# Softcap attention and gated FFN: the weights' sign word from GpSimd, end rows loaded from ScalarE's queue

## The chip, the cores and the metric

The kernel runs on one core of a Trainium2 chip. The metric is the device time of one execution in microseconds (us); less is better. Times of executions that are compared come from the same chip.

## What is computed

A softcapped attention over 4 batches, 12 heads, 448 positions and 64 dimensions feeds a gated FFN over the 1792 tokens (768 wide, 1536 hidden). The weights of the FFN are float64 in memory.

```python
scores = cap * np.tanh(scale * np.matmul(q, k.transpose(0, 1, 3, 2)) / cap)
attn = np.exp(scores - np.max(scores, axis=-1, keepdims=True))
attn = attn / (np.sum(attn, axis=-1, keepdims=True) + 1e-09)
x = np.matmul(attn, v)            # then heads side by side: (1792, 768)
out = (1 / (1 + np.exp(-(x @ w_gate))) * (x @ w_val)) @ w_out
```

## The kernel before

**Stages.** `_emit` runs two generators against each other. `attention_of` (here `_bounded_attention`, since the cap is 30) makes the attention of a batch in 6 pairs of heads; `moe(b)` makes the FFN of batch b. Batch 0's attention runs alone; then moe(0) beside the attention of batch 1, and so on, and moe(3) alone. TensorE and ScalarE take their instructions in the order in which the two generators emit them; the order on VectorE, GpSimd and SP's DMA queue is a scheduler's, with some operations raised in priority.

**Pairs.** For a pair n the scores come out transposed, keys on the partitions; ScalarE takes tanh (L416) and exp (L424). Pairs 0 to 11 (`direct`) multiply float32 tiles; pairs 6 to 11, batch 1, have their keys in 4 chunks of 112 (`even`), the others in chunks of 128. From pair 12 on the exponentials are split into a rounded part `ph` and a remainder `pl` (`emit_P`, L426 to L444), and `a` is summed by GpSimd (L436 to L438). Before that the buffers of tags ph and pl hold only pair 0's transposed k and q. T is the split of the transposed k and q of the next pair: ScalarE rounds it (L209), VectorE makes the remainder (L215), and the next pair's scores wait for it. L530 and L534 or L538 divide by the sum.

**Weights.** There are 36 units of 128 x 768: 24 of w_gate and w_val in turn, 12 of w_out. Each is loaded once as float64 (`load_w64`, L754) and made into float32 in `convert_w` by one ScalarE and three VectorE operations:

```python
nc.scalar.activation(x, top.bitcast(F32), AF.Copy, scale=2.0 ** -112)
nc.vector.tensor_scalar(xi, xi, 3, None, ALU.logical_shift_left)
nc.vector.scalar_tensor_tensor(xi, top, -2 ** 31, xi, ALU.bitwise_and, ALU.bitwise_or)
nc.vector.scalar_tensor_tensor(half, low.bitcast(U32), 2.0 ** -29, half, ALU.mult, ALU.add)
```

They are L771 to L774, on one of two buffers in `pair0`. `split_w` then makes wspl, the rounded part by GpSimd (L207) and the remainder by VectorE (L215; by GpSimd for the first 4 units). `prepare_w(u)` asks for the conversion of unit u + 5. Units 0 to 3 are converted in batch 0's attention at pairs 2 to 5 (`PLAN`), the others in moe(0), one after the other as TensorE reaches unit u; all are stored to memory and loaded again by SP for the later batches (L836, L845), into four wspl buffers, or, for some odd units, as one float32 tile that ScalarE and VectorE split again.

**FFN.** In moe(b), f counts 12 blocks; per block two units (gate, value) of 18 matmuls each (L900), ScalarE's tanh (L943), VectorE's product (L946) and its split into g_spl. Then 12 units of w_out, in two halves of the columns, in three chunks of 128 rows (L1028). The last 64 rows of a batch don't fill a chunk: batches 0 to 2 store their part of g_spl as grest (L959), and the last batch puts all batches' ends into `rest`, four tiles in the buffers of tag t, as two more chunks. At the start of moe(3) the loads rest <- grest (L917), three for each tile, go out on SP's queue; the scheduler has them among SP's loads of batch 2's last weights.

Of the kernel before, what the change touches and what calls it, by code (L numbers as in the profile page):

```python
# [9 lines left out]
F32 = mybir.dt.float32  # L10
F32R = mybir.dt.float32r
I32 = mybir.dt.int32
# [4 lines left out]
ALU = mybir.AluOpType  # L17
AX = mybir.AxisListType

P = 128  # L20
# [230 lines left out]
def _bounded_attention(o, x_done):  # L251
# [13 lines left out]

    nc, c, ap = o.nc, o.c, o.ap
    o.early = 4
    o.out_tag = ("v_spl", 2)
    o.rest_tags = (("t", 2, 2), ("t", 2, 2))
    B, H, S, D, NF, NC, R = o.B, o.H, o.S, o.D, o.NF, o.NC, o.REST  # L270
# [155 lines left out]
    def emit_P(n, j):  # L426

        t = Pt[n][:, j]
        ph = ap.tile([P, NC, S], F32R, tag="ph", bufs=1, name=f"ph{n}_{j}")
        pl = ap.tile([P, NF, S], F32R, tag="pl", bufs=1, name=f"pl{n}_{j}")  # L430
# [8 lines left out]
        f = a[0:D]  # L439
# [181 lines left out]
def _general_attention(o, x_done):  # L621

    nc, c, ap = o.nc, o.c, o.ap
    o.early = 36
    o.out_tag = ("T", 2)
# [7 lines left out]
    for n in range(o.B * o.NPAIR):  # L633
        b, p = divmod(n, o.NPAIR)
# [68 lines left out]
def _emit(tc, ctx, c, attention_of, q, k, v, w_gate, w_val, w_out, out):  # L703
    nc = tc.nc
# [7 lines left out]
    W64 = 3  # L712
    WRAW = 2
    KEEP = 4
    AHEAD = 3
# [16 lines left out]
    UN = KD * P  # L732
# [24 lines left out]
    def convert_w(u):  # L757
# [13 lines left out]
        nc.scalar.activation(x, top.bitcast(F32), AF.Copy, scale=2.0 ** -112)  # L771
        nc.vector.tensor_scalar(xi, xi, 3, None, ALU.logical_shift_left)
        nc.vector.scalar_tensor_tensor(xi, top, -2 ** 31, xi, ALU.bitwise_and, ALU.bitwise_or)
        nc.vector.scalar_tensor_tensor(  # L774
# [118 lines left out]
    def moe(b):  # L893
# [14 lines left out]
        if b == B - 1:  # L908
            tiles = []
            for tag, bufs, n in o.rest_tags:  # L910
                r = ap.tile([P, n, 2, NR // P, KR, P], F32R, tag=tag, bufs=bufs, name=f"rest{len(tiles)}")
                tiles += [r[:, i] for i in range(n)]
            for x, r in enumerate(tiles):
                for at, d in enumerate(g_rest):
                    n = P if at < b // GR else b % GR * R
                    for i in (range(2) if n < P else [slice(0, 2)]):
                        nc.sync.dma_start(  # L917
                            out=r[:, i, at, :, 0:n].bitcast(F32),
                            in_=d[:, i, x * KR:(x + 1) * KR, 0:n].bitcast(F32),
                        )  # L920
                rest.append(r)
        u = u0

        for f in range(KF):
# [8 lines left out]
            for which in range(2):  # L933
# [10 lines left out]
                else:  # L944
                    with tc.high_priority(offset=AHEAD_OF):
                        nc.vector.scalar_tensor_tensor(gate, gate, 1.0, ps, ALU.add, ALU.mult)  # L946
                    o.hi("p", g_spl[:, 0, f, :], gate)
                    o.lo("v", g_spl[:, 1, f, :], gate, g_spl[:, 0, f, :])
        moe1_done[b] = True
        flush_x()  # L950
# [155 lines left out]
```

## Time and profile before

| | |
|---|---|
| runs shown | 760.33, 760.93, 762.32 us; median 760.93 |
| profiled execution, its own time | 760.87 us |
| its span, first to last instruction | 759.1 us |
| mean granted TensorE clock | 0.994 of full speed |
| TensorE busy, matmuls | 742.4 us, 98% |
| VectorE / ScalarE / GpSimd busy | 510.0 / 356.1 / 248.3 us (67 / 47 / 33%) |
| moved by DMA | 151.78 MB, 200 GB/s |

Times in the profile count from the start of the span. Batch 0's attention fills about 0 to 72 us, moe(0) 72 to 265, moe(1) to 435, moe(2) to 601, moe(3) to the end. A matmul's end is modelled, so a busy TensorE is not one at its peak; a share is a mean over stages with different limits. Line numbers are those of the kernel before.

### The profile page before, as it was taken

The numbers are of one execution on the slowest core, as the hardware profiler recorded it, in microseconds if no ns is written. First come the engines' busy times: TensorE is split into PE (matmuls) and PEld (weight loads), VectorE is DVE, ScalarE is ACT, GpSimd is POOL, SyncE is SP. The second block draws the span as 40 slices with busy tenths as digits, with TensorE's granted clock in tenths as the row PEclk, the third lists the DMA queues.
The fourth block names the chain that finished last, engine by engine and source line by source line (L and its number), as shares of the span: only waits on it lengthen the run. The fifth ranks groups of instructions, "written<-read, shape, count | busy, mean of one in ns | idle before, by whom it ended". The sixth has DMA issues, their size and how long they took to land.

```text
span 759.1 us, 10351 instructions
## 1 busy us (share of the span) xinstructions
PE 742.4 (98%) x3900; PEld 642.1 (85%) x3900; DVE 510.0 (67%) x538; ACT 356.1 (47%) x392; POOL 248.3 (33%) x255
## 2 busy tenths in 40 slices
PE   8999999999999799999999999999999999999997
PEld 6556877777788788888899988888998999999996
DVE  3798889978997748988986738899878032322000
ACT  5987565465537156755574155655561011111000
POOL 1364332323333435454545305455462000000000
PEclk9999999999999899999999999999999999999999
DMA  5878798988799674544566854533369855463551
GB/s 127 216 194 214 273 300 264 300 244 264 236 286 349 223 265 118 153 151 139 156 174 224 296 198 134 144 106 123 125 195 307 303 171 176 158 190 103 175 168 57
DMA packets 128391, 151.78 MB, mean 200 GB/s; under 512 B 80716, under 2 KB 106828, under 8 KB 128332
## 3 DMA queue, kind: packets, MB, share of 16 engines
q1 hardware_dynamic: 125468, 147.02, 61.9%
q10 hardware_dynamic: 2864, 4.00, 1.5%
q8 instruction: 33, 0.54, 0.3%
q14 instruction: 26, 0.21, 0.1%
HBM read 118.75 MB, written 31.46 MB: 198 GB/s over the span
## 4 chain that ended last, share of the span: by engine, by line
PE 63%; DMA 2%; DVE 1%; SPq 0%; issue 0%; ACT 0%
PE h L900 35%; PE o L1028 17%; PE sc L413 4%; DMA wspl<-wd 2%; PE pv L484 2%; PE pv L483 2%; PE dn L522 1%; PE pv L485 1%; PE tp L360 1%; PE tp L244 1%; DVE rd L530 0%; SPq L845 0%; DVE ph L215 0%; DVE wspl L215 0%; DVE a L440 0%
## 5 line engine op out<-in xcount | busy, mean ns | idle before, releaser
L900 PE MATMUL h<-xspl,wspl 128*128 128x448 f32 x1728 | 377.1, 372 | 0.0
L900 PEld LDWEIGHTS h<-xspl,wspl 128*128 128x128 f32 x1728 | 321.3, 188 | 41.7 <-issue 15.5
L1028 PE MATMUL o<-wspl,gspl 128*128 128x384 f32 x864 | 162.8, 342 | 6.3 <-DVE wspl L215 3.9
L1028 PEld LDWEIGHTS o<-wspl,gspl 128*128 128x128 f32 x864 | 152.7, 190 | 12.2 <-DVE wspl L215 4.2
L416 ACT ACTIVATE t<-sc,scale 128x896 f32<-128x896 f32 (+1 forms) x90 | 85.9, 1002 | 32.5 <-PE sc L413 32.2
L207 POOL TENSOR_SCALAR gspl<-gate 128x448 fp32r<-128x448 f32 x48 | 43.1, 897 | 162.2 <-DVE gate L946 162.2
L424 ACT ACTIVATE t<-t,capv 128x1792 f32<-128x1792 f32 (+2 forms) x48 | 83.2, 1738 | 10.1 <-issue 6.4
L215 DVE TENSOR_TENSOR wspl<-pair,wspl 128x768 fp32r<-128x768 f32 x68 | 76.9, 1132 | 15.0 <-POOL wspl L207 12.5
L946 DVE SCALAR_TENSOR_TENSOR gate<-gate,h 128x448 f32<-128x448 f32 x48 | 29.6, 616 | 74.1 <-PE h L900 64.1
L943 ACT ACTIVATE gate<-h 128x448 f32<-128x448 f32 x48 | 26.1, 543 | 105.6 <-PE h L900 105.1
L530 DVE RECIPROCAL rd<-rd 128x448 f32<-128x448 f32 x24 | 70.7, 2947 | 5.1 <-ACT rd L503 2.7
L413 PE MATMUL sc<-T 64*128 64x448 f32 (+1 forms) x522 | 66.5, 382 | 1.1 <-DVE T L215 1.1
L207 POOL TENSOR_SCALAR wspl<-pair 128x768 fp32r<-128x768 f32 x36 | 35.5, 986 | 94.1 <-DVE pair L774 48.3
L413 PEld LDWEIGHTS sc<-T 64*128 64x128 f32 (+1 forms) x522 | 44.9, 181 | 20.7 <-issue 11.8
L209 ACT ACTIVATE wspl<-pair 128x768 fp32r<-128x768 f32 x36 | 30.4, 844 | 66.7 <-PE h L900 66.5
L436 POOL TENSOR_TENSOR a<-t 128x448 f32<-128x448 f32 x24 | 31.3, 1304 | 67.4 <-ACT t L424 32.3
L1002 DVE TENSOR_SCALAR osb<-o 128x384 f32<-128x384 f32 x16 | 8.6, 555 | 62.8 <-PE o L1028 62.7
L209 ACT ACTIVATE ph<-t 128x1792 fp32r<-128x1792 f32 x24 | 40.8, 1698 | 14.0 <-PE pv L485 14.0
L215 DVE TENSOR_TENSOR pl<-t,ph 128x1344 fp32r<-128x1344 f32 x24 | 46.3, 1929 | 0.4
L215 DVE TENSOR_TENSOR gspl<-gate,gspl 128x448 fp32r<-128x448 f32 x48 | 41.3, 860 | 7.2 <-POOL gspl L207 6.9
L774 DVE SCALAR_TENSOR_TENSOR pair<-w,pair 128x768 uint16<-128x768 uint32 x36 | 41.7, 1161 | 0.4
L771 ACT ACTIVATE pair<-w 128x768 f32<-128x768 f32 x36 | 32.4, 908 | 19.7 <-DVE wspl L215 18.2
(92 smaller groups left out, 762.7 us busy)
## 6 DMA issues: line engine op xcount, KB each, us to landing
wspl<-wd SPq DMA_DIRECT2D x72, 768.0 KB, 5.6
wd<-wspl SPq DMA_DIRECT2D x20, 768.0 KB, 5.7
pair<-wr SPq DMA_DIRECT2D x36, 384.0 KB, 3.1
w<-in_moe_w_gate_dram SPq DMA_DIRECT2D x12, 768.0 KB, 7.0
w<-in_moe_w_val_dram SPq DMA_DIRECT2D x12, 768.0 KB, 6.3
w<-in_moe_w_out_dram SPq DMA_DIRECT2D x12, 768.0 KB, 5.8
qk<-in_q_dram SPq DMA_DIRECT2D x44, 112.0 KB, 4.6
wr<-pair SPq DMA_DIRECT2D x12, 384.0 KB, 4.5
```

The costliest lines, as they stand in the source:

```text
L207: self.nc.gpsimd.tensor_scalar(dst, src, 1.0, 1.0, ALU.mult, ALU.mult)
L209: self.nc.scalar.activation(dst, src, AF.Copy)
L215: e.tensor_sub(dst, src, hi.bitcast(F32))
L413: nc.tensor.matmul(ps[0:w, j, 0:S], a[rows], r[rows], start=(i == 0), stop=(i == len(ops) - 1))
L416: nc.scalar.activation(Pt[n][0:w, :, m, :], ps[0:w, :, 0:S], AF.Tanh, scale=c["scale"][0:w])
L424: nc.scalar.activation(t, t, AF.Exp, scale=c["cap"][rows])
L436: nc.gpsimd.tensor_add(a, t[:, 0, :], t[:, 1, :])
L530: nc.vector.reciprocal(rd, rd)
L771: nc.scalar.activation(x, top.bitcast(F32), AF.Copy, scale=2.0 ** -112)
L774: nc.vector.scalar_tensor_tensor(half, low.bitcast(U32), 2.0 ** -29, half, ALU.mult, ALU.add)
L900: nc.tensor.matmul(ps, a, r, start=(kk == 0 and i == 0), stop=(kk == KD - 1 and i == 2))
L1028: nc.tensor.matmul(ps, a, r, start=(y + kk == 0 and i == 0), stop=(y + kk == KF - 1 and i == 2),)
```

## The change

Three things stand in its title. The sign word: L772 goes; instead GpSimd multiplies the scaled word by zero, which leaves a zero with the sign, into a tile `sg` in the buffer of tag ph or pl in turn, and one VectorE operation shifts and joins. `sign_tags` is emptied at the first `emit_P` and in the other attention, where the old two operations stand. End rows: the loads rest <- grest go out on ScalarE's queue, one tile's three loads after each of the blocks f = 4 to 7 of the last batch. Batch 1 in chunks of 112 keys: `even` has it so before and after; the diff has no line on it.

```diff
--- before.py
+++ after.py
@@ -264,6 +264,7 @@
 
 
     nc, c, ap = o.nc, o.c, o.ap
+    o.sign_tags = ("ph", "pl")
     o.early = 4
     o.out_tag = ("v_spl", 2)
     o.rest_tags = (("t", 2, 2), ("t", 2, 2))
@@ -426,6 +427,7 @@
     def emit_P(n, j):
 
         t = Pt[n][:, j]
+        o.sign_tags = ()
         ph = ap.tile([P, NC, S], F32R, tag="ph", bufs=1, name=f"ph{n}_{j}")
         pl = ap.tile([P, NF, S], F32R, tag="pl", bufs=1, name=f"pl{n}_{j}")
         o.hi("a", ph, t)
@@ -621,6 +623,7 @@
 def _general_attention(o, x_done):
 
     nc, c, ap = o.nc, o.c, o.ap
+    o.sign_tags = ()
     o.early = 36
     o.out_tag = ("T", 2)
     o.rest_tags = (("t", 2, 1), ("t", 2, 1), ("pt", 2, 1), ("pt", 2, 1))
@@ -711,6 +714,7 @@
     KU = 2
     W64 = 3
     WRAW = 2
+    REST_AT = 4
     KEEP = 4
     AHEAD = 3
     WB = 4
@@ -769,8 +773,16 @@
         xi = x.bitcast(I32)
         half = x.bitcast(U16).rearrange("p (n t) -> p n t", t=2)[:, :, 0]
         nc.scalar.activation(x, top.bitcast(F32), AF.Copy, scale=2.0 ** -112)
-        nc.vector.tensor_scalar(xi, xi, 3, None, ALU.logical_shift_left)
-        nc.vector.scalar_tensor_tensor(xi, top, -2 ** 31, xi, ALU.bitwise_and, ALU.bitwise_or)
+        if o.sign_tags:
+            tag = o.sign_tags[conv["next"] % len(o.sign_tags)]
+            sg = o.ap.tile([P, UN], F32, tag=tag, bufs=1, name=f"sg{u}")
+            nc.gpsimd.tensor_scalar(sg, x, 0.0, None, ALU.mult)
+            nc.vector.scalar_tensor_tensor(
+                xi, xi, 3, sg.bitcast(I32), ALU.logical_shift_left, ALU.bitwise_or
+            )
+        else:
+            nc.vector.tensor_scalar(xi, xi, 3, None, ALU.logical_shift_left)
+            nc.vector.scalar_tensor_tensor(xi, top, -2 ** 31, xi, ALU.bitwise_and, ALU.bitwise_or)
         nc.vector.scalar_tensor_tensor(
             half, low.bitcast(U32), 2.0 ** -29, half, ALU.mult, ALU.add
         )
@@ -910,15 +922,17 @@
             for tag, bufs, n in o.rest_tags:
                 r = ap.tile([P, n, 2, NR // P, KR, P], F32R, tag=tag, bufs=bufs, name=f"rest{len(tiles)}")
                 tiles += [r[:, i] for i in range(n)]
-            for x, r in enumerate(tiles):
-                for at, d in enumerate(g_rest):
-                    n = P if at < b // GR else b % GR * R
-                    for i in (range(2) if n < P else [slice(0, 2)]):
-                        nc.sync.dma_start(
-                            out=r[:, i, at, :, 0:n].bitcast(F32),
-                            in_=d[:, i, x * KR:(x + 1) * KR, 0:n].bitcast(F32),
-                        )
-                rest.append(r)
+            rest += tiles
+
+        def load_rest(x):
+            for at, d in enumerate(g_rest):
+                n = P if at < b // GR else b % GR * R
+                for i in (range(2) if n < P else [slice(0, 2)]):
+                    nc.scalar.dma_start(
+                        out=rest[x][:, i, at, :, 0:n].bitcast(F32),
+                        in_=d[:, i, x * KR:(x + 1) * KR, 0:n].bitcast(F32),
+                    )
+
         u = u0
 
         for f in range(KF):
@@ -946,6 +960,8 @@
                         nc.vector.scalar_tensor_tensor(gate, gate, 1.0, ps, ALU.add, ALU.mult)
                     o.hi("p", g_spl[:, 0, f, :], gate)
                     o.lo("v", g_spl[:, 1, f, :], gate, g_spl[:, 0, f, :])
+            if 0 <= f - REST_AT < len(rest):
+                load_rest(f - REST_AT)
         moe1_done[b] = True
         flush_x()
```

How it moves instructions, at three places. Names are the tiles', with the number of the pair, unit or batch in them; in the rows of the change lines are numbered as in the changed file (L780 is the new shift and join, L786 the old L774, L532 the old L530, L536 L534, L540 L538, L931 L917).

VectorE in batch 0's attention, from the reciprocal of pair 2 to T of pair 5, before:

```order
L530 RECIPROCAL rd2_481<-rd2_481 128x448
L534 SCALAR_TENSOR_TENSOR xraw0_311<-pv2_0_436,rd2_481 64x448
L534 SCALAR_TENSOR_TENSOR xraw0_311<-pv2_1_438,rd2_481 64x448
L772 TENSOR_SCALAR pair0_66<-pair0_66 128x768
L773 SCALAR_TENSOR_TENSOR pair0_66<-w64_2_174,pair0_66 128x768
L774 SCALAR_TENSOR_TENSOR pair0_66<-w64_2_174,pair0_66 128x768
L215 TENSOR_TENSOR T5_553<-tp5_544,T5_553 128x960
```

and in the change:

```order
L532 RECIPROCAL rd2_483<-rd2_483 128x448
L536 SCALAR_TENSOR_TENSOR xraw0_311<-pv2_0_438,rd2_483 64x448
L536 SCALAR_TENSOR_TENSOR xraw0_311<-pv2_1_440,rd2_483 64x448
L780 SCALAR_TENSOR_TENSOR pair0_66<-pair0_66,sg2_518 128x768
L786 SCALAR_TENSOR_TENSOR pair0_66<-w64_2_174,pair0_66 128x768
L215 TENSOR_TENSOR T5_556<-tp5_547,T5_556 128x960
```

GpSimd there in the change:

```order
L327 MEMSET vo4_492 128x8x64
L779 TENSOR_SCALAR sg2_518<-pair0_66 128x768
L207 TENSOR_SCALAR xspl0_2_489<-xraw0_311 128x448
L215 TENSOR_TENSOR xspl0_2_489<-xraw0_311,xspl0_2_489 128x448
L207 TENSOR_SCALAR wspl2_522<-pair0_66 128x768
L215 TENSOR_TENSOR wspl2_522<-pair0_66,wspl2_522 128x768
```

L772 is gone, and GpSimd's new pass sg2, on which L780 waits, stands ahead of its work on x of pair 2, which is unchanged; the memset ahead of it stood there before.

VectorE at the end of moe(0), from unit 34's remainder to unit 35's (wspl35), before:

```order
L215 TENSOR_TENSOR wspl34_2187<-pair0_66,wspl34_2187 128x768
L773 SCALAR_TENSOR_TENSOR pair0_66<-w64_35_2049,pair0_66 128x768
L774 SCALAR_TENSOR_TENSOR pair0_66<-w64_35_2049,pair0_66 128x768
L215 TENSOR_TENSOR pl12_0_2200<-t12_2022,ph12_0_2199 128x1344
L215 TENSOR_TENSOR ph12_0_2199<-t12_2022,ph12_0_2199 64x448
L440 TENSOR_TENSOR a12_0_2204<-a12_0_2204 64x448
L530 RECIPROCAL rd11_2115<-rd11_2115 128x448
L215 TENSOR_TENSOR wspl35_2229<-pair0_66,wspl35_2229 128x768
L215 TENSOR_TENSOR as12_0_2209<-a12_0_2204,as12_0_2209 64x448
L538 SCALAR_TENSOR_TENSOR xraw1_924<-xraw1_924,rd11_2115 128x448
```

and in the change:

```order
L215 TENSOR_TENSOR wspl34_2223<-pair0_66,wspl34_2223 128x768
L215 TENSOR_TENSOR ph12_0_2235<-t12_2054,ph12_0_2235 64x448
L780 SCALAR_TENSOR_TENSOR pair0_66<-pair0_66,sg35_2219 128x768
L532 RECIPROCAL rd11_2149<-rd11_2149 128x448
L786 SCALAR_TENSOR_TENSOR pair0_66<-w64_35_2082,pair0_66 128x768
L215 TENSOR_TENSOR pl12_0_2236<-t12_2054,ph12_0_2235 128x1344
L442 TENSOR_TENSOR a12_0_2240<-a12_0_2240 64x448
L540 SCALAR_TENSOR_TENSOR xraw1_933<-xraw1_933,rd11_2149 128x448
L215 TENSOR_TENSOR wspl35_2265<-pair0_66,wspl35_2265 128x768
```

The remainder of ph and the reciprocal of pair 11 have moved up, and L538 of pair 11 now stands ahead of wspl35; the sum a and pl stand behind the conversion as before.

SP's queue in batch 2's output stage, before (units 98 to 103 are batch 2's units 26 to 31):

```order
L845 DMA wspl98_4961<-wd26_1812 128x1536
L917 DMA rest0_5370<-grest0_1850 128x2x384 x2
L836 DMA pair0_66<-wr7_855 128x768
L959 DMA grest2_5020<-gspl2_3923 3072x1x64
L845 DMA wspl100_5086<-wd28_1910 128x1536
L845 DMA wspl101_5088<-wd29_1962 128x1536
L917 DMA rest0_5370<-grest2_5020 128x3x64 x4
L845 DMA wspl102_5122<-wd30_1993 128x1536
L845 DMA wspl103_5150<-wd31_2054 128x1536
L917 DMA rest2_5371<-grest0_1850 128x2x384
L917 DMA rest2_5371<-grest2_5020 128x3x64 x2
```

ScalarE in the last batch, in the change:

```order
L209 ACTIVATE wspl119_5604<-pair0_66 128x768
L957 ACTIVATE gate3_4_5603<-h3_0_4_5607 128x448
L931 DMA rest0_5406<-grest0_1878 128x2x384
L931 DMA rest0_5406<-grest2_5056 128x3x64 x2
L209 ACTIVATE wspl121_5656<-pair0_66 128x768
L957 ACTIVATE gate3_5_5655<-h3_0_5_5659 128x448
L931 DMA rest0_5406<-grest0_1878 128x2x384
L931 DMA rest0_5406<-grest2_5056 128x3x64 x2
L209 ACTIVATE wspl123_5708<-pair0_66 128x768
```

All twelve loads of rest have left SP's rows and stand between the gates on ScalarE; the other two tiles follow in blocks 6 and 7 in the same way. SP's other rows there keep their order. Elsewhere on SP some loads of w64 and of q and k change places by a few rows; in moe(0) the load of unit 32's w64 now stands behind the last four loads of pair 14's k and q.

## Rows read from the trace of the kernel before

**Rows 1.** Waits of TensorE: engine, line, releaser: us in total, times, longest.

```profile
PE o L1028 <- DVE wspl L215: 3.9, 1, 3.9
PE o L1028 <- DMA wspl<-wd: 1.8, 2, 1.3
...
PE sc L413 <- DVE T L215: 1.1, 4, 0.4
```

**Rows 2.** Busy time by stretch: length, PE, PEld, DVE, ACT, POOL; clock, DMA share, GB/s.

```profile
40.00:60.00 20.00, 19.54 (x96) 11.22 (x95) 19.34 (x18) 18.27 (x20) 12.03 (x11) 1.00 0.83 210
256.00:260.00 4.00, 0.28 (x1) 0.28 (x2) 3.97 (x3) 0.00 (x0) 0.56 (x1) 0.75 0.00 0
260.00:264.00 4.00, 4.00 (x13) 4.00 (x14) 1.57 (x3) 0.52 (x2) 0.56 (x1) 0.50 0.87 270
580.00:602.00 22.00, 20.20 (x114) 19.48 (x114) 6.17 (x7) 1.09 (x2) 0.56 (x1) 1.00 0.90 314
```

**Rows 3.** Groups by line on VectorE: count | busy us, mean ns | idle before.

```profile
L530 DVE RECIPROCAL rd<-rd 128x448 f32<-128x448 f32 x24 | 70.7, 2947 | 5.1 <-ACT rd L503 2.7 <-ACT rd L527 1.9
...
L772 DVE TENSOR_SCALAR pair<-pair 128x768 int32<-128x768 int32 x36 | 21.1, 585 | 4.5 <-ACT pair L771 4.3
...
L538 DVE SCALAR_TENSOR_TENSOR xraw<-xraw,rd 128x448 f32<-128x448 f32 x18 | 15.0, 834 | 0.3
```

**Rows 4.** Timeline, batch 0, conversions of units 1 and 2: start, length, engine, line.

```profile
36.91 0.90 ACT L771 ACTIVATE pair<-w 128x768 f32<-128x768 f32 x1
...
38.57 0.56 DVE L772 TENSOR_SCALAR pair<-pair 128x768 int32<-128x768 int32 x1
...
47.32 0.90 ACT L771 ACTIVATE pair<-w 128x768 f32<-128x768 f32 x1 [0.38 <-issue]
...
48.34 0.56 DVE L772 TENSOR_SCALAR pair<-pair 128x768 int32<-128x768 int32 x1
...
48.94 1.20 DVE L773 SCALAR_TENSOR_TENSOR pair<-w,pair 128x768 int32<-128x768 int32 x1
...
49.41 1.72 POOL L215 TENSOR_TENSOR xspl<-xraw,xspl 128x448 fp32r<-128x448 f32 x1
...
50.17 1.85 DVE L774 SCALAR_TENSOR_TENSOR pair<-w,pair 128x768 uint16<-128x768 uint32 x1
...
51.92 1.14 DVE L215 TENSOR_TENSOR T<-tp,T 128x960 fp32r<-128x960 f32 x1
...
52.11 0.83 POOL L207 TENSOR_SCALAR wspl<-pair 128x768 fp32r<-128x768 f32 x1 [0.98 <-DVE pair L774]
```

**Rows 5.** Timeline at the end of moe(0), units 34 and 35.

```profile
245.80 1.71 ACT L209 ACTIVATE ph<-t 128x1792 fp32r<-128x1792 f32 x1
...
247.09 1.91 DVE L215 TENSOR_TENSOR wspl<-pair,wspl 128x768 fp32r<-128x768 f32 x1
...
248.27 1.74 POOL L437 TENSOR_TENSOR a<-a,t 128x448 f32<-128x448 f32 x1
...
248.92 1.90 DVE L773 SCALAR_TENSOR_TENSOR pair<-w,pair 128x768 int32<-128x768 int32 x1
...
255.92 2.94 DVE L530 RECIPROCAL rd<-rd 128x448 f32<-128x448 f32 x1
...
258.78 0.89 DVE L215 TENSOR_TENSOR wspl<-pair,wspl 128x768 fp32r<-128x768 f32 x1
...
259.72 5.72 PE L1028 MATMUL o<-wspl,gspl 128*128 128x384 f32 x18 [3.91 <-DVE wspl L215]
```

**Rows 6.** Timeline, batch 2's output stage; last, from the chain, batch 3's f blocks.

```profile
582.16 3.72 SPq L917 DMA_DIRECT2D rest<-grest  x3
...
585.98 9.06 SPq L845 DMA_DIRECT2D wspl<-wd  x4
...
588.16 7.58 PE L1028 MATMUL o<-wspl,gspl 128*128 128x384 f32 x42 [1.30 <-DMA wspl<-wd]
...
601.72 89.28 PE h L900 x432
```

## The prediction

> **What bounds the kernel now.** I read three views in this order: who waited for whom on TensorE, the stretches around those waits, and the timeline there. TensorE is the bound nearly throughout, so a saving counts only where TensorE waits, and there are three such places. One wait of 3.9 us for the low part of a weight unit (L215), two waits of 1.8 us in all for weight loads, and four waits of 1.1 us in all for a T tile [rows 1]. The reader should match each with its place.
>
> The wait of 3.9 us is at 255.8, for unit 35, the last weight converted beside batch 0's FFN [rows 5]. It costs more than its length: the granted clock reads 0.75 in 256 to 260 and 0.50 in 260 to 264, which is the 1.2 GHz level after TensorE stood idle [rows 2]. The 18 matmuls from 259.72 took 5.72 us; 42 of the same kind took 7.58 [rows 5, 6], 0.18 each, so 18 are worth 3.25. The clock costs 2.5 us, the place 6.4.
>
> The two waits for loads are in 580 to 602, while the clock stays at 1.00 [rows 2, 6]. SP issued three of the twelve loads of end rows at 582.16, needing 3.72 us, and only at 585.98 the weight loads behind them; TensorE stood 1.30 us at 588.16 [rows 6].
>
> The four waits for T are in batch 0's attention, where VectorE is busy 19.34 of 20 us and TensorE 19.54 [rows 2]: both are nearly full, and VectorE ends last, by the 0.28 us that TensorE waits on average in each of four pairs [rows 1].
>
> **The change part by part.** *The sign word.* Per unit VectorE loses L772 (0.585 us, 36 of them, 21 us in all) and keeps two operations of the old kind [rows 3]; GpSimd gains one pass over 128x768, for which I take the 0.83 us of its pass over the same tile at 52.11 [rows 4]. The catch is how the two engines share. L773 issued at 248.92 ran 1.90 us where the same size took 0.89 at 258.78; GpSimd's add held from 248.27 to 250.01, and 250.01 plus 0.81 is 250.82, where L773 ended [rows 5]. So they take turns, and a sign pass beside a VectorE operation with two SBUF inputs costs VectorE up to 0.83 where 0.585 was saved.
> The Trainium skill, "SBUF — State Buffer", section "Who interferes with whom", says this as a rule: a VectorE instruction with two SBUF inputs and a GpSimd instruction that reads SBUF exclude each other for a whole instruction. That row agrees; by the rule a sign pass gains nothing where VectorE is always busy, and the sum would be that of rival C, 764.3, in place of 758.9.
>
> *Where that matters, batch 0.* Four units are converted there, one per pair. In the pair shown, L772 starts at 48.34, and T's low part 3.58 us later, at 51.92, with L773, L774 and GpSimd's passes over x taking turns between [rows 4]. Now the sign pass starts when ScalarE's L771 has ended (48.22) and GpSimd has seen it (0.09 us, as from L774's end at 52.02 to 52.11), and ends at 49.14, 0.80 after 48.34. The rest runs as before less L772's 0.56: T starts 0.24 us later. In the pair ahead of it L771 ended at 37.81, well before L772's start at 38.57 [rows 4]; there the same sum is 37.81 + 0.92 - 38.57 - 0.56, so T starts 0.40 us earlier. Since TensorE waits for T, a delay goes through whole and a gain up to the 0.28. I take +0.1 for each of the four pairs, **+0.4 us**, nearer the later pair since ScalarE's own row does not move. Ends: the four waits vanish (-1.1), or every pass costs its whole length (4 x 0.83 = +3.3).
>
> *The other 32 units.* TensorE waits once in the run for a converted unit, unit 35 [rows 1]; the others are ready before their use, so what they gain or lose is hidden by TensorE's own matmuls until that lead is used up. What counts is unit 35. Its place in VectorE's order changes: pair 11's reciprocal, which followed both of its conversions, now stands between them; L538 moves ahead of its last operation; and ph's low part stands ahead of its first, so the whole list waits for ScalarE's ph (now 245.80 to 247.51) [rows 5]. Before, from the end of unit 34's low part (249.00) to the end of unit 35's (259.67) VectorE needed 10.67 us. Now L538 joins (+0.83 [rows 3]), while the reciprocal, which kept 2.94 us, falls beside GpSimd's adds in place of one or two conversions that ran at double length (-0.95 to -1.9). That leaves 9.6 to 10.6 us; I take 10.1, the middle. The list starts at the later of unit 34's end and ph's, which I put at 249.0: L772 is gone, but ph is held up by L771 of unit 35, which waits for unit 33. So unit 35 ends at 259.1 instead of 259.67: **-0.6 us**. A start between 247.5 and 251 gives -2.6 to +1.9, and the upper end of the gain adds the clock's 2.5. TensorE's order is unchanged, so the wait stays about 3.3 us and the clock still falls.
>
> *End rows.* The twelve loads leave SP's queue in batch 2's output stage; SP's weight loads behind them go out up to 3.7 us earlier, against waits of 1.3 and (1.8 less 1.3) 0.5. I take the whole **-1.8 us** [rows 1]; ends 0 and -1.8. They land on ScalarE's queue, three in each of four f blocks of batch 3. A block takes 7.44 us (89.28 for 432 matmuls, 18 per unit, two units [rows 6]). Three issues cost ScalarE at most 3.7 us by SP's price, and the next gate is due a block later, so I cost it at nothing; what hides it is TensorE's matmuls of that block. If ScalarE had to wait for earlier transfers before each issue, the cover would end at 7.44 us a block; that is rival D's second half.
>
> *The rest.* Chunks of 112 keys for batch 1 are in the kernel before already; no line of the diff touches them: 0. The sign buffers are ph and pl, idle until pair 12; all 36 passes stand ahead of pair 12's use: 0. On SP some loads of w64 swap with loads of q and k; unit 32's weights go out behind four of them; no row shows TensorE waiting for these, so I cost it at nothing, within the bounds of unit 35.
>
> **Sum.** The profiled execution took 760.87 us (759.1 of span and 1.8 around it), the median of the three runs 760.93, so both are the same base. 760.87 + 0.4 - 0.6 - 1.8 = **758.9 us**. A measurement of this kernel can tell about 0.3% from no change, 2.3 us here, so "faster" begins below 758.65 and "slower" above 763.2.
>
> **The rivals.** *A, the forecast:* 757.1 to 761.1, chance 0.52. The small terms cannot be told apart from zero; the end rows are the firm part.
>
> *B, the clock does not fall.* If VectorE's relief reaches unit 35 and the wait shrinks to about 1.5 us, the idle time is like that of 588.16 (1.30), after which the clock stayed up. For it: 21 us leave a VectorE that is busy 3.97 of 4 us in 256 to 260 [rows 2, 3]. Against it: the new order and ScalarE's part in the list. Time: 760.87 + 0.4 - 1.8 - 2.4 - 2.5 = 754.6; with no wait left, 1.5 less, 753.1. Chance 0.20.
>
> *C, slower: the shared turn decides.* Each sign pass costs VectorE its whole 0.83 us. In batch 0 that is +3.3, and at the end, where GpSimd does the passes of units 32 to 35 ahead of the high parts of older units, the list of unit 35 starts at 251, the late end above (+1.9). It decides when T starts over 4.4 us after L534 (3.58 + 0.83). Time: 760.87 + 3.3 + 1.9 - 1.8 = 764.3. For it: L773's 1.90. Against it: a pass beside the reciprocal takes no turn from it, whose 2.94 us at 255.92 is also its mean over all 24 [rows 3, 5]; and in the pair at 38.57 the pass is nearly over before VectorE is free. Chance 0.17.
> [...]
>
> *D, the end rows' gain is not there.* The weight loads may be late for another reason (SP also issues the stores of the output), or ScalarE holds a gate up. Time: 760.87 + 0.4 - 0.6 = 760.7. Chance 0.11. Against it: these two waits are the only ones for weight loads in the run, and only this stage has the end rows on SP.
>
> **How the numbers follow.** Of A, about 0.23 lies below 758.65 and 0.29 above; B is faster, C slower, D the same. Faster 0.23 + 0.20 = 0.43, same 0.29 + 0.11 = 0.40, slower 0.17. The range 754.0 to 764.3 leaves out the lower part of B and the upper half of C.
>
> **What would show it.** Right: no TensorE wait on weight loads in 580 to 602; T between 0.4 us earlier and 0.24 us later after L534; unit 35 ready within a microsecond of 259.7 and the clock again at 0.50 for some microseconds. Wrong: no stretch at 0.50 (B); T over 4.4 us after L534 and several new waits on VectorE (C); waits for weight loads still there (D); or a wait of TensorE in batch 3's f blocks 4 to 8, which would come from ScalarE's queue.

## The result and the profile after

The changed kernel takes 772.28 us (median of 4 runs, 771.27 to 772.62), the kernel before 760.88 on the same chip: 1.5% slower, ratio 1.0145 with a 95% interval of 1.0127 to 1.0162, some 11.4 us. The forecast was 758.9 and its range ended at 764.3. The profiled execution has a span of 770.4 us against 759.1.

The groups by line come first: the sign pass on GpSimd, the pass of GpSimd over the same tile that makes the high part, VectorE's new join, and ScalarE's conversion that opens each unit.

```profile
L779 POOL TENSOR_SCALAR sg<-pair 128x768 f32<-128x768 f32 x36 | 85.7, 2381 | 23.6 <-ACT pair L775 23.6
L207 POOL TENSOR_SCALAR wspl<-pair 128x768 fp32r<-128x768 f32 x36 | 39.8, 1104 | 39.9 <-issue 10.6 <-DVE pair L786 7.0 <-PE h L912 6.4
...
L780 DVE SCALAR_TENSOR_TENSOR pair<-pair,sg 128x768 int32<-128x768 int32 x36 | 45.0, 1250 | 23.1 <-POOL sg L779 23.0
...
L775 ACT ACTIVATE pair<-w 128x768 f32<-128x768 f32 x36 | 32.7, 910 | 66.8 <-DVE wspl L215 64.1 <-DMA wr<-pair 2.7
```

The sign pass takes 2381 ns on average, where the forecast had 0.83 us; the other pass, of the same shape, takes 1104. VectorE stands 23.0 us before the joins until the sign word is there. ScalarE stands 64.1 us before conversions until the low part of an older unit (wspl, L215) is done; before the change that was 18.2:

```profile
L771 ACT ACTIVATE pair<-w 128x768 f32<-128x768 f32 x36 | 32.4, 908 | 19.7 <-DVE wspl L215 18.2 <-DMA wr<-pair 0.6 <-DMA w<-in_moe_w_val_dram 0.5
```

TensorE's waits after the change, which answer to [rows 1]:

```profile
PE o L1044 <- DVE wspl L215: 4.3, 1, 4.3
PE sc L414 <- DVE T L215: 4.1, 3, 1.9
PE o L1044 <- ACT osb L1020: 2.4, 1, 2.4
PE pv L476 <- ACT xraw L507: 2.4, 2, 1.6
PE tp L244 <- ACT t L417: 2.1, 2, 1.6
...
PE o L1044 <- DVE gate L960: 1.6, 1, 1.6
```

The waits for weight loads (1.8 us) are gone; those for T grew from 1.1 to 4.1; and five waits on ScalarE (for osb, xraw and t), 6.9 us in all, stand where before there was one of 0.5.

How the time divides shows in the starts of the first h matmul of each FFN stage and of the last matmul of the run (us):

| | moe(0) begins | to moe(1) | to moe(2) | to moe(3) | to the end |
|---|---|---|---|---|---|
| before | 72.2 | 194.6 | 169.2 | 165.6 | 151.5 |
| after | 76.7 | 203.9 | 169.4 | 162.8 | 151.5 |

Batch 0's attention lost 4.5 us, moe(0) 9.4, and the stage with the end rows gained 2.8: 11.3 with the 0.2 between. The loss lies only where units are converted.

**Batch 0.** The timeline of unit 2's conversion, over ScalarE, GpSimd, VectorE and TensorE:

```profile
49.92 1.27 DVE L536 SCALAR_TENSOR_TENSOR xraw<-pv,rd 64x448 f32<-64x448 f32 x2
50.02 0.89 ACT L775 ACTIVATE pair<-w 128x768 f32<-128x768 f32 x1
51.00 2.13 POOL L779 TENSOR_SCALAR sg<-pair 128x768 f32<-128x768 f32 x1 [2.99 <-ACT pair L775]
...
53.17 1.30 DVE L780 SCALAR_TENSOR_TENSOR pair<-pair,sg 128x768 int32<-128x768 int32 x1 [1.99 <-POOL sg L779]
...
56.26 1.15 DVE L215 TENSOR_TENSOR T<-tp,T 128x960 fp32r<-128x960 f32 x1
...
57.45 1.28 PE L414 MATMUL sc<-T 64*128 64x448 f32 x10 [1.86 <-DVE T L215]
```

VectorE is free at 51.19 and stands idle until 53.17. T, queued behind the join, starts at 56.26, 5.07 us after xraw's end, where the forecast's limit for its slower rival was 4.4. Except in its first 0.19 us the pass has an idle VectorE beside it, and it still takes 2.13 us: no turn-taking is in it. Not all of the 4.5 us is the pass's: in the five other profiled kernels with this pass in batch 0 moe(0) begins at 74.8 to 75.2, so 2.6 to 3.0 us recur, and the rest goes with a fall of the clock that only this profile has (last section).

**moe(0).** ScalarE is held at its conversions, and what is queued behind them reaches TensorE late. ScalarE's and TensorE's timelines at two such places:

```profile
157.91 0.90 ACT L775 ACTIVATE pair<-w 128x768 f32<-128x768 f32 x1 [5.03 <-DVE wspl L215]
...
159.84 1.88 ACT L417 ACTIVATE t<-sc,scale 112x896 f32<-112x896 f32 x2
...
160.89 0.98 PE L244 MATMUL tp<-ident,qk 112*128 112x112 f32 x8 [1.61 <-ACT t L417]
...
247.52 0.91 ACT L775 ACTIVATE pair<-w 128x768 f32<-128x768 f32 x1 [5.50 <-DVE wspl L215]
248.33 1.24 ACT L1020 ACTIVATE osb<-o 128x384 f32<-128x384 f32 x3
...
248.86 3.13 PE L1044 MATMUL o<-wspl,gspl 128*128 128x384 f32 x12 [2.45 <-ACT osb L1020]
```

Raw units have two places in pair0. Each is free only when the low part of the unit in it is done, and that end now comes later by the sign pass. ScalarE therefore stands 5.03 and 5.50 us at the next conversion, while the tanh (t) and the output (osb) that TensorE needs are queued behind. Of moe(0)'s 9.4 us, TensorE's waits there account for 7.8: 1.6 for t, 2.4 for xraw, 2.4 for osb, 1.6 for the gate and 4.3 for unit 35, together 12.3, less 3.9 and 0.6 of the same kind before. The granted clock falls behind these pauses, as in [rows 2]:

```profile
248.00:252.00 4.00, 3.14 (x13) 2.97 (x14) 2.97 (x3) 3.95 (x8) 3.02 (x2) 0.78 0.93 271
...
272.00:276.00 4.00, 1.42 (x4) 1.42 (x5) 3.83 (x5) 0.00 (x0) 1.85 (x3) 0.76 0.53 218
```

The clock falls at two places in moe(0) now (252 to 256 reads 0.80 and 276 to 280 reads 0.81 as well), where before it fell at one, but further, to 0.50. Whether the 1.6 us that are not in the waits are this stays open.

### The profile page after: what moved, and what is told of

Same layout as the page of the kernel before. It is cut to its first block, busy times and chain, and to the rows that moved or that the text cites. A ratio compares the mean times of both kernels' runs of the same rounds, so it can differ in the third digit from the quotient of the medians.

```text
span 770.4 us, 10333 instructions
## 1 busy us (share of the span) xinstructions
PE 745.0 (97%) x3900; PEld 644.2 (84%) x3900; DVE 504.4 (65%) x502; ACT 356.0 (46%) x392; POOL 329.2 (43%) x291
## 4 chain that ended last, share of the span: by engine, by line
PE 68%; DVE 4%; ACT 3%; POOL 2%; issue 1%; DMA 1%; ACTq 0%; DVEq 0%
PE h L912 38%; PE o L1044 19%; PE sc L414 4%; PE pv L486 2%; PE pv L485 2%; POOL sg L779 2%; PE pv L476 1%; DVE wspl L215 1%; ACT pair L775 1%; DVE pair L780 1%; DMA w<-in_moe_w_out_dram 1%; ACT t L425 1%; PE pv L487 1%; PE dn L524 1%; PE tp L244 1%
## 5 line engine op out<-in xcount | busy, mean ns | idle before, releaser
L1044 PEld LDWEIGHTS o<-wspl,gspl 128*128 128x128 f32 x864 | 152.5, 190 | 13.4 <-DVE wspl L215 4.6
L207 POOL TENSOR_SCALAR gspl<-gate 128x448 fp32r<-128x448 f32 x48 | 36.3, 755 | 145.0 <-DVE gate L960 144.9
L779 POOL TENSOR_SCALAR sg<-pair 128x768 f32<-128x768 f32 x36 | 85.7, 2381 | 23.6 <-ACT pair L775 23.6
L215 DVE TENSOR_TENSOR wspl<-pair,wspl 128x768 fp32r<-128x768 f32 x68 | 76.9, 1131 | 14.7 <-POOL wspl L207 11.9
L532 DVE RECIPROCAL rd<-rd 128x448 f32<-128x448 f32 x24 | 70.7, 2947 | 5.9 <-ACT rd L505 3.6
L775 ACT ACTIVATE pair<-w 128x768 f32<-128x768 f32 x36 | 32.7, 910 | 66.8 <-DVE wspl L215 64.1
L780 DVE SCALAR_TENSOR_TENSOR pair<-pair,sg 128x768 int32<-128x768 int32 x36 | 45.0, 1250 | 23.1 <-POOL sg L779 23.0
L207 POOL TENSOR_SCALAR wspl<-pair 128x768 fp32r<-128x768 f32 x36 | 39.8, 1104 | 39.9 <-issue 10.6
L215 DVE TENSOR_TENSOR gspl<-gate,gspl 128x448 fp32r<-128x448 f32 x48 | 44.3, 924 | 6.7 <-POOL gspl L207 6.4
```

Source lines behind the costliest of these rows:

```text
L207: self.nc.gpsimd.tensor_scalar(dst, src, 1.0, 1.0, ALU.mult, ALU.mult)
L215: e.tensor_sub(dst, src, hi.bitcast(F32))
L532: nc.vector.reciprocal(rd, rd)
L779: nc.gpsimd.tensor_scalar(sg, x, 0.0, None, ALU.mult)
L780: nc.vector.scalar_tensor_tensor(xi, xi, 3, sg.bitcast(I32), ALU.logical_shift_left, ALU.bitwise_or)
L1044: nc.tensor.matmul(ps, a, r, start=(y + kk == 0 and i == 0), stop=(y + kk == KF - 1 and i == 2),)
```

## The experiments

Theory 1: the sign pass costs 2.1 us and more because it is written with one operation, and its length is the loss. Theory 2: GpSimd is slow because the engines get in each other's way. Theory 3: the end rows, ScalarE's queue or the new order of instructions cost. The groups' lines are those of each kernel's own file. Each ratio is to the kernel before on the same chip; a time set against that of another run can be from another chip (the kernel before took 760.8 to 761.7 us on them), so where a microsecond counts the ratio decides.

**The same pass with two operations** (sign_twoop, sign_twoop_again).

```diff
-            nc.gpsimd.tensor_scalar(sg, x, 0.0, None, ALU.mult)
+            nc.gpsimd.tensor_scalar(sg, x, 0.0, 1.0, ALU.mult, ALU.mult)
```

> The change with its sign pass written with two operations (times 0.0, then times 1.0) instead of one, as the pass over the same tile that makes the high part is written; nothing else differs. Theory 1 (the one-operation form is what makes the pass 2381 ns, and those passes are the loss): the pass falls to 0.8 to 1.1 us, the wait of VectorE for it (23.0 us in all after the change) falls under 5 us, and the time to 757 to 761 us. Theory 2 (GpSimd is slow here because VectorE's joins and ScalarE's conversions work on the same tiles at the same time): the pass stays at 2.1 us or more and the time within 2 us of 772. Theory 3 (the loss comes from the moved end rows or from the changed order): the pass gets shorter, but the time stays at 768 or more.

Measured: 755.34 us, ratio to before 0.9907 (0.9877 to 0.9937), and in the second series 757.42, 0.9958 (0.9945 to 0.9972). Of the first series the joins' group, the sign pass by its line (shortest, median and longest in ns, first and last start), two of TensorE's waits, and the end of moe(0):

```profile
L780 DVE SCALAR_TENSOR_TENSOR pair<-pair,sg 128x768 int32<-128x768 int32 x36 | 41.3, 1151 | 14.0 <-POOL sg L779 13.8
```

```profile
L779 POOL TENSOR_SCALAR sg<-pair x36: 827/855/1623, 28.6 to 244.8; 128x768 f32<-128x768 f32 x36
```

```profile
PE sc L414 <- DVE T L215: 1.9, 3, 0.7
PE h L912 <- DMA wspl<-wd: 1.8, 1, 1.8
```

```profile
256.00:260.00 4.00, 4.00 (x25) 3.93 (x23) 3.87 (x4) 0.98 (x2) 0.16 (x1) 1.00 0.72 210
```

The pass falls to a median of 855 ns, the time by 16.9 and 14.9 us (by the ratios 2.4 and 1.9%). The first series lies below the 757 to 761 us expected. VectorE's waits for the pass stay at 13.8, above the 5 us expected, and cost TensorE little: its waits for T are 1.9 us, against 1.1 before and 4.1 in the change. Unit 35's wait is gone and the clock stays at 1.00, where it fell before [rows 2]. The wait of 1.8 us for weights, at the begin of moe(1), is new. Theory 1 stands in its main point. What differs beside the length is the order of VectorE's, GpSimd's and SP's instructions, which the builder sets by its own estimates; hence the next run.

**A short pass in the change's order** (sign_copy).

```diff
-            nc.gpsimd.tensor_scalar(sg, x, 0.0, None, ALU.mult)
+            nc.gpsimd.tensor_copy(sg, x)
```

> The change with the sign pass replaced by GpSimd's plain copy of the same tile, so that the sign word holds the whole word and the output is not the reference's. The copy took 0.83 us alone in the price list, and with it PE's and ScalarE's instructions stand exactly as in the change, VectorE's nearly so (11 of 1756 rows elsewhere before the last units, against 55 in the two-operation form). Theory 1 (the pass's length is the loss): 755 to 760 us. Rival (the two-operation form gains because its instructions stand in another order): 765 us or more.

Measured: 757.69 us, 0.9953 (0.9936 to 0.9971). Here unit 35 is waited for about as forecast, and the clock falls, to 0.79 where the forecast had 0.50:

```profile
PE o L1044 <- DVE wspl L215: 3.0, 1, 3.0
```

```profile
256.00:260.00 4.00, 1.36 (x4) 1.36 (x5) 3.83 (x5) 0.00 (x0) 1.90 (x3) 0.79 0.77 277
```

In almost the change's order a pass of 828 ns (median) gives a result 14.6 us below the change. The length is what costs; the order makes the difference of whether unit 35 waits (3.0 us here, none in the two-operation form), which the two results, 0.9953 against 0.9907 and 0.9958, do not tell apart in the total.

**What of the form is slow** (sign_f32r, sign_bypass, prices).

```diff
-            sg = o.ap.tile([P, UN], F32, tag=tag, bufs=1, name=f"sg{u}")
+            sg = o.ap.tile([P, UN], F32R, tag=tag, bufs=1, name=f"sg{u}")
```

> The change with the sign word's tile declared as TensorE's rounded type, as the high part's tile is, the pass still with one operation. Theory 1 (the number of operations sets the pass's price): the pass stays at 2.1 to 2.4 us and the time at 772. A rival (the type of the output sets it): the pass falls to about 1 us and the time to about 759.

```diff
-            nc.gpsimd.tensor_scalar(sg, x, 0.0, None, ALU.mult)
+            nc.gpsimd.tensor_scalar(sg, x, 0.0, 1.0, ALU.mult, ALU.bypass)
```

> The change with a second scalar and bypass written as the second operation; every engine's instructions stand as in the change. If what is slow is a pass whose second operation is bypass: 2.1 us or more per pass and 770 to 774 us. If what is slow is the missing second scalar: 0.83 us and 755 to 760 us.

```diff
-        o.hi("p" if u < NU else "a", s[:, 0, :], t)
+        if u >= NU:
+            o.hi("a", s[:, 0, :], t)
+        elif u % 4 == 0:
+            nc.gpsimd.tensor_scalar(s[:, 0, :], t, 1.0, None, ALU.mult)
+        elif u % 4 == 1:
+            nc.gpsimd.tensor_scalar(s[:, 0, :], t, 0.0, None, ALU.add)
+        elif u % 4 == 2:
+            nc.gpsimd.tensor_copy(s[:, 0, :], t)
+        else:
+            o.hi("p", s[:, 0, :], t)
```

> The kernel with the end rows moved and VectorE's old sign word, in which GpSimd's 36 passes that make the high part are written in four forms by turns: times 1.0 in one operation, plus 0.0 in one operation, a copy, and times 1.0 twice as now. Theory 1 in its plain form (one operation is slow, whatever it is): the first two at 2.1 us or more, the last at 0.83 us where nothing runs beside it, and the copy unknown. A rival (only multiplication by zero, or only the multiplication, is slow): one of the first two at about 0.83 us.

With the other output type the pass kept a median of 2138 ns (one run, 770.36 us), with a written bypass 2136 (770.77 us). The price list, by form:

```profile
L831 POOL TENSOR_SCALAR wspl<-pair 128x768 fp32r<-128x768 f32 x9 | 21.8, 2427 | 8.1 <-DVE pair L786 6.1 <-PE h L921 2.0
L829 POOL TENSOR_SCALAR wspl<-pair 128x768 fp32r<-128x768 f32 x9 | 21.5, 2384 | 28.9 <-DVE pair L786 17.8 <-PE h L921 5.6 <-DMA w<-in_moe_w_out_dram 5.5
...
L833 POOL CAST wspl<-pair 128x768 fp32r<-128x768 f32 x9 | 9.5, 1054 | 22.5 <-DVE pair L786 13.8 <-PE h L921 5.3 <-PE o L1053 3.4
...
L207 POOL TENSOR_SCALAR wspl<-pair 128x768 fp32r<-128x768 f32 x9 | 9.1, 1008 | 17.6 <-DVE pair L786 11.0 <-PE h L921 4.4 <-PE o L1053 2.1
```

L829 multiplies by 1.0, L831 adds 0.0, each with one operation: 2384 and 2427 ns, the shortest 2141 and 2142. The copy (L833) and the pass with two multiplications take 1054 and 1008. So neither the zero, the multiplication nor the output's type is slow, but a scalar pass over this tile whose second operation is none or bypass. That kernel ran 757.25 us (one run): 18 slow passes at this place cost nothing that one run can show. Yet ScalarE stood 40.6 us before conversions there until an older unit's low part was done, against 17.8 in rest_only, while TensorE waited 1.3 us for ScalarE in all. So holding ScalarE does not cost by itself; it costs where TensorE waits for what stands behind.

**The parts of the change alone** (sign_only, rest_only). sign_only is the change with the loop `for x, r in enumerate(tiles)` on `nc.sync` put back; rest_only is the change with

```diff
-    o.sign_tags = ("ph", "pl")
+    o.sign_tags = ()
```

> The change without the move of the end rows, which are loaded on SP's queue again as before; the sign word stays with GpSimd in one operation. Theory 1 (the sign pass is the loss, the end rows give back 1.8 us): 773 to 775 us, with the two waits for weight loads near 600 us back. Theory 3 (the end rows or ScalarE's queue take part in the loss): under 770 us.

> The kernel before with the end rows alone moved to ScalarE's queue; the sign word is made by VectorE as before. Theory 1: 758 to 760 us, the 1.8 us of waits for weight loads near 600 us gone. Theory 3 (the end rows or ScalarE's queue take part in the loss): 762 us or more.

Measured: sign_only 773.02 us, 1.0151 (1.0122 to 1.0180); rest_only 758.81, 0.9963 (0.9946 to 0.9980). The end rows' move is a gain by itself, and the stage before moe(3) takes 162.8 us in rest_only as in the change, 164.4 in sign_only and 165.6 before. In sign_only the waits for weight loads are back with 1.0 us, not 1.8, and the move is worth 1.6 us of that stage, in rest_only 2.8. Theory 3 falls for the end rows.

**Where the passes cost** (sign_split, sign_late). In sign_split the first four units keep the one-operation pass; in sign_late they keep VectorE's old steps; all others have two operations.

```diff
-            nc.gpsimd.tensor_scalar(sg, x, 0.0, None, ALU.mult)
+            if u < KEEP:
+                nc.gpsimd.tensor_scalar(sg, x, 0.0, None, ALU.mult)
+            else:
+                nc.gpsimd.tensor_scalar(sg, x, 0.0, 1.0, ALU.mult, ALU.mult)
```

> The change with the sign pass in one operation for the four units that are converted in batch 0, and in two operations for the 32 of the first expert stage. The change and its two-operation form differ by 16.9 us in all; in their profiles the first matmul of the expert stage starts at 76.7 and 72.7 us. Theory 1a (the loss adds up place by place, four passes on batch 0's path and the rest in the expert stage): 758.5 to 760.5 us, which is 4 us over the two-operation form. Rival 1b (the time lost in batch 0 is taken back later, because a later start finds its loads and units further on): 755 to 757 us.

```diff
-        if o.sign_tags:
+        if o.sign_tags and u >= KEEP:
```

> The two-operation form, with VectorE's old two steps for the four units converted in batch 0. The term that the prediction set for batch 0 was a loss of 0.4 us. If that is right: 754.5 to 755.3 us. If the freed 0.585 us of VectorE counts there (a gain in batch 0): 756 to 757.5 us. If GpSimd in batch 0 costs more than was set: under 754.3 us.

> The two-operation form once more, with more rounds, to set it against the form that leaves batch 0's four units with VectorE (756.64 us). If batch 0 costs nothing with the 0.83 us pass: 755 to 757 us; the first matmul of the expert stage at 72.7 us again.

sign_split took 759.21 us, 0.9969 (0.9955 to 0.9983): 3.9 and 1.8 us over the two series of the two-operation form. By the profiles four slow passes in batch 0 cost 2.5 to 2.9 us (moe(0) begins at 75.2 against 72.7 and 72.3), and moe(0) gives little of it back: it takes 190.7 us in sign_split, 190.8 and 191.6 in the other form. Theory 1a stands, with a smaller sum than the 4 us, part of which was the clock (last section). sign_late took 756.64, 0.9932 (0.9914 to 0.9951), between the two series of the two-operation form; moe(0) begins at 72.8 us in it. That time lies in the branch of a gain (756 to 757.5), but with 2.1 us between two series of the same kernel no branch can be told from another; by where moe(0) begins (72.8 against 72.7 and 72.3) the short pass changes batch 0 by at most 0.5 us.

**ScalarE held at its conversions** (raw3_oneop, raw3_twoop): a third place for raw units, in the idle tile of tag pl, and all sign words in tag ph.

```diff
-        at = conv["next"] % WRAW * UN
-        x = c["pair0"][:, at:at + UN]
+        at = conv["next"] % 3
+        if at < 2 or not o.sign_tags:
+            at = conv["next"] % (3 if o.sign_tags else 2) * UN
+            x = c["pair0"][:, at:at + UN]
+        else:
+            x = o.ap.tile([P, UN], F32, tag="pl", bufs=1, name=f"raw{u}")
...
-            tag = o.sign_tags[conv["next"] % len(o.sign_tags)]
+            tag = "ph"
```

> The change with its slow one-operation sign pass, and a third place for raw units: every third unit that is converted lies in the tile of the low parts of P (idle then), and the sign word always in the tile of the high parts. Theory M (in the expert stage the slow pass costs because ScalarE stands at a conversion until one of two raw places comes free, 64.1 us in the change against 18.2 before, and TensorE then waits for what ScalarE does next: t 2.1, xraw 2.4, osb 2.4 us): ScalarE's wait falls under 30 us, those three waits of TensorE under 2 us in all, and the time to 765 to 768 us. Rival (the pass costs by VectorE's own waits for it, 23.0 us, whatever ScalarE does): the time stays within 2 us of 772.

> The two-operation form with the third place for raw units. ScalarE's wait for a raw place is 17.6 us in the two-operation form and TensorE's waits for ScalarE 0.5 us, so theory M leaves little to gain: 754 to 756 us. If the waits for the last unit's weights (0.7 us before the output stage of batch 0) or of the next stage still hang on conversions: 752 to 754 us.

raw3_oneop took 765.94 us, 1.0076 (1.0057 to 1.0095). ScalarE's two groups of conversions and TensorE's waits:

```profile
L779 ACT ACTIVATE pair<-w 128x768 f32<-128x768 f32 x24 | 21.8, 908 | 36.6 <-DMA w<-in_moe_w_out_dram 21.8 <-DMA w<-in_moe_w_gate_dram 14.8
L779 ACT ACTIVATE raw<-w 128x768 f32<-128x768 f32 x12 | 11.0, 914 | 14.6 <-DMA w<-in_moe_w_gate_dram 9.0 <-DMA w<-in_moe_w_out_dram 4.7 <-DMA w<-in_moe_w_val_dram 0.7
```

```profile
PE sc L414 <- DVE T L215: 3.9, 4, 1.8
PE o L1048 <- DVE gate L964: 3.5, 1, 3.5
...
PE o L1048 <- ACT osb L1024: 1.4, 1, 1.4
```

No wait for a raw place is left: what ends ScalarE's pauses is now the load of the next unit. TensorE's waits on ScalarE shrink from 6.9 us to 2.3 (osb 1.4, t 0.5 and 0.4), a little over the 2 expected, and moe(0) from 203.9 to 198.0, with the slow pass unchanged (2475 ns). VectorE's own waits for the sign word, which the rival makes the cause, did not shrink, 23.4 us against 23.0:

```profile
L784 DVE SCALAR_TENSOR_TENSOR pair<-pair,sg 128x768 int32<-128x768 int32 x24 | 31.2, 1302 | 12.4 <-POOL sg L783 12.4
...
L784 DVE SCALAR_TENSOR_TENSOR raw<-raw,sg 128x768 int32<-128x768 int32 x12 | 15.3, 1272 | 11.0 <-POOL sg L783 11.0
```

So the rival falls, and the hold is worth some 5.9 of the 9.4 us of moe(0). The longest wait left in moe(0) is 3.5 us for a gate, which was not followed further. Batch 0 ends at 75.2, as in sign_only (75.1), so some 1.5 us of the gain on the change are the clock of its profile. With the short pass the third place (raw3_twoop) gave 754.59 us, 0.9928 (0.9910 to 0.9945), the best ratio beside sign_twoop's first series and on its chip 2.8 us below the two-operation form.

**A pass that nobody reads** (dead_oneop, dead_twoop), added to rest_only.

```diff
+        if o.sign_tags:
+            if u == 0:
+                c["dead"] = o.ap.tile([P, UN], F32, tag="pl", bufs=1, name="dead")
+                nc.vector.memset(c["dead"], 1.0)
+            nc.gpsimd.tensor_scalar(c["dead"], c["dead"], 0.0, None, ALU.mult)
```

> The kernel with the end rows moved and VectorE's old sign word, to which a pass of GpSimd in one operation (times 0.0, in place on a tile of its own that nobody reads) is added at the place of each of the 36 sign passes. Nobody waits for its result; GpSimd is busy with it for 36 times 2.1 us. Theory 1 (the change loses because VectorE's join waits for a pass of 2.4 us): within 3 us of the kernel without the added pass, 758 to 762 us, what is lost being passes that stand behind it on GpSimd. Theory 2 (a long pass of GpSimd by itself slows VectorE's operations, by the port that they share): 766 us or more, with VectorE's operations on the same shapes 15% longer or more.

> The kernel with the end rows moved and VectorE's old sign word, with the added pass that nobody reads, this time in two operations. Its one-operation form cost 7.4 us (766.16 against 758.81). Theory 1 (what cost was the pass's length on GpSimd's queue): 758 to 760 us, the pass at 0.83 to 1.1 us. Rival (any added pass beside VectorE costs, by the port that they share): 762 us or more.

dead_oneop took 766.16 us, 1.0058 (1.0039 to 1.0077); dead_twoop 762.55, 1.0027 (1.0016 to 1.0039). The dead passes do not run where the sign passes do (28.8 to 262.8 us in the change): they wait for nothing, and all 36 are done by 150.0 us in dead_oneop and by 65.9, within batch 0, in dead_twoop. The time of dead_oneop meets theory 2 and misses theory 1; all of the loss is in moe(0) (202.5 us against 195.3; it begins at 71.6 against 72.8). Theory 2's reason holds in part: VectorE's joins of the old kind took 1149 ns on average against 1135 in rest_only, where other passes lengthen them, but the twelve beside a dead pass alone have a median of 1.45 us, those beside no pass 0.96; the shift pass took 752 ns against 598. The longest new wait, 3.2 us, is near moe(0)'s begin. TensorE's row first, then GpSimd's and VectorE's:

```profile
81.13 1.32 PE L909 MATMUL h<-xspl,wspl 128*128 128x448 f32 x3 [3.16 <-DVE xspl L215]
...
74.17 2.14 POOL L780 TENSOR_SCALAR dead<-dead 128x768 f32<-128x768 f32 x1
76.27 0.87 POOL L207 TENSOR_SCALAR xspl<-xraw 128x448 fp32r<-128x448 f32 x1
77.11 4.79 POOL L780 TENSOR_SCALAR dead<-dead 128x768 f32<-128x768 f32 x2
...
77.48 2.44 DVE L782 SCALAR_TENSOR_TENSOR pair<-w,pair 128x768 int32<-128x768 int32 x2
79.84 1.24 DVE L215 TENSOR_TENSOR xspl<-xraw,xspl 128x448 fp32r<-128x448 f32 x1
```

The last xraw is ready at 74.87, its high part goes out only behind a dead pass, at 76.27, and its low part behind two joins on VectorE, at 79.84. So a long pass costs here by what is queued behind it; how much of the 7.4 us is this and how much VectorE's longer passes was not separated. In batch 0, by contrast, sixteen long passes that nobody reads cost nothing, which fits a loss of the change there by the join's wait for the word.

dead_twoop missed theory 1's 758 to 760 and reaches its rival's 762. It loses in batch 0 alone (moe(0) begins at 75.6 against 72.8 and takes 194.7 against 195.3), where all its dead passes are, so it says nothing of short passes in moe(0). They push GpSimd's add over the unit into VectorE's next conversion:

```profile
48.91 0.85 POOL L780 TENSOR_SCALAR dead<-dead 128x768 f32<-128x768 f32 x1
49.72 2.14 POOL L215 TENSOR_TENSOR wspl<-pair,wspl 128x768 fp32r<-128x768 f32 x1
51.83 1.54 POOL L780 TENSOR_SCALAR dead<-dead 128x768 f32<-128x768 f32 x1
...
50.21 2.46 DVE L782 SCALAR_TENSOR_TENSOR pair<-w,pair 128x768 int32<-128x768 int32 x1
```

VectorE's join, 1.20 us before [rows 4], takes 2.46 between them, and TensorE's waits for T come to 4.5 us. The Trainium skill, "SBUF — State Buffer", section "Who interferes with whom", has this as the rule that a VectorE instruction with two SBUF inputs and a GpSimd instruction that reads SBUF exclude each other; these rows agree. Beside a one-operation pass the whole-length turn does not show, here in the change:

```profile
250.06 2.13 POOL L779 TENSOR_SCALAR sg<-pair 128x768 f32<-128x768 f32 x1
250.13 1.57 DVE L215 TENSOR_TENSOR wspl<-pair,wspl 128x768 fp32r<-128x768 f32 x1 [0.73 <-POOL wspl L207]
```

VectorE's low part, 0.95 us with nothing beside it, is 0.62 us longer, but ends 0.49 us before the pass. So theory 2 is a real cost where passes pile up beside VectorE, and not what made this change's pass long. The two dead kernels' orders differ as well, so they don't give one price for both.

## Why the prediction was wrong

**The step that failed is the price of the sign pass,** "for which I take the 0.83 us of its pass over the same tile at 52.11 [rows 4]". That row is on the same engine, tile and shape, but L207 is written with two operations and the sign pass with one. It measured 2.13 us with VectorE idle, 2.38 on average. The upper end of the range was built on 0.83 as well ("every pass costs its whole length (4 x 0.83 = +3.3)"), so no case held the price itself open. The trace of before had no one-operation pass of GpSimd, and it had a dearer row over the same tile, the add of 1.84 us, which could have served as an upper bound. With it rival C's +3.3 for batch 0 would have been 4 x 1.84 = +7.4, and the range would have ended at 768.4: nearer, and still short, since the loss in moe(0) goes a way that no term had.

**Batch 0** was +0.4 us and lost 4.5, of which 2.6 to 3.0 recur in other kernels with the pass. With the short pass the term holds: T starts 3.78 us after xraw's end in the two-operation form (48.16 to 51.94), 0.2 later than before, as forecast for the later pair (0.24), and moe(0) begins at 72.7 and 72.3 against 72.2.

**The other 32 units** "are ready before their use, so what they gain or lose is hidden by TensorE's own matmuls until that lead is used up". In the change TensorE waits for none of them either, so the first half holds; the second fails, and this is the second step that failed: a term put at nothing, where moe(0) lost 9.4 us. What it left out is who else waits for a unit's end: ScalarE, for the raw place, with batch 1's tanh, xraw and the output tile behind it (64.1 us of holding against 18.2; a third place gave back 5.9 us of moe(0)). "ScalarE's own row does not move" is true of batch 0 only.

**Unit 35** was to be 0.6 us earlier with a wait of about 3.3 and a falling clock. With a short pass in nearly this order (sign_copy) the wait is 3.0 and the clock falls, though to 0.79 and not to 0.50, so the working holds in the main; in the change the wait is 4.3 us.

**End rows:** -1.8 us taken whole; the waits are gone, and the stage is 2.8 us shorter (165.6 to 162.8); rest_only's ratio says 0.2 to 0.5%. The step holds, a little small. TensorE does not wait in batch 3's f blocks, and moe(3) takes 151.5 us before and after, so ScalarE's queue cost nothing there.

**The rivals.** C named the sign that came true, T over 4.4 us after xraw, but its reason, a shared turn, did not: VectorE was idle beside the pass, and where it works beside one the turn is shorter than the pass (250.13, above). C's other sign, several new waits on VectorE, came in part: T and the gate wait longer, the other new waits are on ScalarE. B, the clock that does not fall, came true in the two-operation form (755.34 and 757.42 for 754.6). D did not occur. Under its own premise of 0.83 us, then, the forecast of 758.9 was 1.2 to 3.6 us too high (757.69, 757.42, 755.34); from these to the measured 772.28 it is 14.6 us and more, and that is the price and where it went. That the miss is only 13.4 us is thus in part the luck of terms that were too dear.

## What to carry to other kernels

A price taken from a row holds for that form of instruction: same engine, shape and type are not enough, and the number of operations in a scalar pass belongs to the form. If the trace has no row of the exact form, the range must hold the price open at least up to the dearest row over the same tile; here even that, 1.84 us, was below the 2.13 measured. And a longer conversion costs not only its consumer: look who waits for its buffer, and what stands behind that one in an in-order queue. Here that was ScalarE, and the work that TensorE needed.

## What the runs showed of the hardware

- GpSimd's scalar pass over 128x768 takes 2.12 us at least with one operation (times 0.0, times 1.0, plus 0.0, or with a written bypass) and 0.83 with two multiplications, 0.82 as a copy. Here the cheaper way to multiply once was to multiply twice.
- Of those 2.12 us only a part holds a VectorE operation with two SBUF inputs: one that starts 0.07 us into the pass takes 1.57 us in place of 0.95 and ends 0.49 us before it (250.13 in the change).
- The same pause of TensorE for T in batch 0 (1.83 us in the change, 1.86 in sign_only) was followed by a lower clock in one profile and not in the other:

```profile
35.19 2.23 PE L414 MATMUL sc<-T 64*128 64x448 f32 x10 [1.83 <-DVE T L215]
```

```profile
35.06 1.29 PE L414 MATMUL sc<-T 64*128 64x448 f32 x10 [1.86 <-DVE T L215]
```

The first row is of the change (granted clock 0.68 in 36 to 40), the second of sign_only (1.00 there); moe(0) begins at 76.7 and 75.1 us. In sign_f32r, sign_bypass, sign_split and raw3_oneop the pause is 1.85 or 1.86 us, the clock 1.00 and the begin of moe(0) 74.8 to 75.2. So the same pause can go either way, and 1.5 to 1.9 us of batch 0's 4.5 go with the clock and not with the pass itself.
